# ReLU-squared attention and SwiGLU on one core: the sums of squares of the norm, taken in f32 on ScalarE and VectorE and closed by one matmul

## The chip, the cores and the metric

One core of a Trainium2 chip runs the whole kernel. The metric is the device time of one execution in microseconds, as the median of several runs. Engines are named as the profile names them: PE (TensorE, with PEld for its weight loads), DVE (VectorE), ACT (ScalarE), POOL (GpSimd), SP (SyncE).

## The reference

Eight batches of twelve heads, 448 positions, head size 64. The attention has no softmax: the scores are rectified, squared and divided by the length. Its output, put back into 3584 rows of 768, goes through an RMS norm and a gated feed-forward block without biases (d_ff 1536).

```python
scores = (q @ k.T) / sqrt(64)
attn = maximum(scores, 0) ** 2 / 448
x = (attn @ v) with heads side by side          # 3584 x 768
rms = sqrt(mean(x * x, axis=-1) + 1e-6)
xn = x / rms * rms_g
out = (silu(xn @ w_gate) * (xn @ w_val)) @ w_out
```

All inputs and the output are f32 in memory; the kernel computes its matmuls in bf16 with f32 sums.

## The kernel before, in words

**Layout.** Features lie on partitions: the attention output of a batch is a tile xT of 128 partitions x 6 feature blocks x 448 positions (a block is a pair of heads). The six blocks of a batch come in three **visits** of two blocks each (`visit_aux`): a visit multiplies the rectified and squared scores by V (psAV, L823, 28 matmuls) into a PSUM tile of two banks. One engine then copies that tile, scaled, into xT in bf16 (L850 on DVE or L848 on ACT), and DVE squares the copy in bf16 (L853) into a tile of squares. Within a visit, between the two parts of its V matmuls, four matmuls make scores of the next visit (psR, L737).

**Order.** Nothing in the program waits for "what is ready": a planner in Python (`Planner`) writes one fixed order for each engine. It keeps an estimated time for each engine, gives each task (a copy, a rectification, a square) a cost per engine, and picks the task or matmul that can start first by these estimates. The engines then run their lists in that order, with semaphores where data or a buffer demands it, so a wait that the planner did not count holds everything behind it on that engine. A task's data are given as tokens (`need`), and a PSUM bank counts as free when the task that was given the bank's release ends.

**PE in two halves.** Most matmuls use 64 of the 128 contraction rows, so that two run side by side: half 0 on the lower and half 1 on the upper 64 rows. A segment (`Seg`) is a sum over several slots, half 0 first, then half 1 added to the same PSUM tile; `slot` (L139) issues them, and while half 1 works on one segment half 0 works on the next. The feed-forward blocks (psg, psv), the output projection (psO) and the sums of squares (psSS) of batches 1 to 7 are such segments. Work that is not a segment is put between slots as an insert (`ins`, `do_ins`): the score units psS (L716), one matmul in each half, are.

**PSUM.** Four single banks serve psg, psv, psO and psSS; two double banks (`wide`) serve psS, psR and psAV, so that a score unit needs one of the two to be free. A psS or psR tile is freed by its rectification on ACT (L661) or DVE (L659); a psAV tile was freed by its copy to xT. The squares of the rectified scores (L667) run on DVE, and for batch 1 the planner could also choose POOL.

**Norm.** After the last visit of a batch, `norm_seg` puts a segment of six slots (one per feature block, weights all ones) ahead in PE's stream: 12 matmuls of 64 rows x 448 positions that sum the squares over all features. ACT takes the logarithm and the exponential (L903, L907) for the reciprocal root, DVE makes xn (L922), and the feed-forward block of the batch starts with it. While that goes on, PE works on the output projection (psO) of batches finished earlier. Batch 0 is done in two halves of 224 positions whose sums (L948) are matmuls of their own.

Of the kernel before, what the change touches and what calls it, by code (L numbers as in the profile page):

```python
# [8 lines left out]
FP32 = mybir.dt.float32  # L9
BF16 = mybir.dt.bfloat16  # L10
# [44 lines left out]
class Planner:  # L55
# [6 lines left out]
    def __init__(self, nc, tc, banks, wide, warm):  # L62
        self.nc, self.tc, self.banks, self.wide, self.warm = nc, tc, banks, wide, warm
        self.free = {"act": 1300.0, "dve": 1500.0, "pool": 1300.0, "sp": 1300.0}
        self.tasks, self.seq = [], 0
        self.t = [1100.0, 1100.0]
        self.mode = "row"
        self.ins = [[], []]
        self.aux = None
        self.cur, self.next0, self.q8 = None, [], []  # L70
        self.stream = []
        self.units, self.auxes = [], []
        self.behind = mybir.DependencyInfo(
            mybir.DependencyClass.Sync, mybir.DependencyReason.DATA
        )
# [138 lines left out]

    def half(self, h):
        t = self.t[h]
        if self.ins[h]:
            return t, lambda: self.do_ins(h)
        if self.aux is not None:
            if h == 0 and not self.ins[1]:  # L220
                return max(self.t), self.do_aux
            return None
        if h == 1:
            if not self.q8:
                return None
            seg = self.q8[0]
            if seg.count[1] == 0:
                if seg.fin[0] is None:
                    return None
                return max(t, seg.fin[0]), lambda: self.slot(1, seg)  # L230
            return t, lambda: self.slot(1, seg)
        return self.choose(t)

    def do_ins(self, h):
        self.row()
        w, emit, cb = self.ins[h].pop(0)
        s = self.t[h]
        emit()
        TRACE.append((s, w / 2.4 + 2.5, "pe%d" % h, "score"))
        self.t[h] = s + w / 2.4 + 2.5  # L240
        if cb:
            cb(s + w / 2.4 + self.PSUM)
# [11 lines left out]
    def choose(self, t):  # L254
        self.auxes = [a for a in self.auxes if not a.void()]
        self.warm()
        for a in self.auxes:
            r = a.ready()
            if r is not None and r <= t:
                return t, lambda: self.set_aux(a)  # L260
        s = self.stream_next(t)
        u = None
        if self.units and not any(a.holds() for a in self.auxes):
            u = self.units[0].ready()
        if u is not None and u <= t and (self.units[0].due() or s is None or s[0] > t):
            return t, self.begin_unit
        if s is not None and s[0] <= t:
            return t, lambda: self.slot(0, s[1])
        times = [s[0]] if s is not None else []
        if u is not None:  # L270
            times.append(u)
        for a in self.auxes:
            r = a.ready()
            if r is not None:
                times.append(r)
        if self.warm() and (not times or min(times) > t + 250.0):
            return t, self.filler
        if not times:
            return None
        at = min(times)  # L280
        return at, lambda: self.skip(at)
# [4 lines left out]
    def set_aux(self, a):  # L286
        self.auxes.remove(a)
        self.aux = a

    def begin_unit(self):  # L290
        self.units.pop(0).begin()
# [8 lines left out]
    def run(self):  # L300
        while True:
            p = None
            for h in (0, 1):
                c = self.half(h)
                if c is not None and (p is None or c[0] < p[0]):
                    p = c
            e = self.engine_next()
            if p is None and e is None:
                break
            if e is not None and (p is None or e[3] <= p[0]):  # L310
                self.run_task(*e[1:])
            else:
                p[1]()
        left = (len(self.stream), len(self.q8), len(self.units), len(self.auxes), len(self.tasks))
        assert not any(left) and self.cur is None, left


# [7 lines left out]
def kernel(  # L325
# [11 lines left out]
    nc = tc.nc  # L337
# [38 lines left out]
    def act_cost(n, per=0.8333):  # L376
        return 172.0 + per * n

    def dve_cost(n, per=1.0417):
        return 156.0 + per * n  # L380
# [260 lines left out]
            return None if any(x is None for x in toks) else latest(toks)  # L641

    live = {"r": 0}
    xTs, x2s, rstds, xns, hTs = {}, {}, {}, {}, {}
    subs = [Sub(0, 0, HALF, 0.0), Sub(0, HALF, HALF, 0.0)]
    subs += [Sub(b, 0, S, 0.0 if b < 2 else PACE) for b in range(1, B)]

# [2 lines left out]
    def rectify(sub, ps, bank, w, ready, put):  # L650

        got = {}
        tok = Tok()

        def relu(e):
            r = apool.tile([P, 2, S], BF16, name="r", tag="r")
            got["r"] = r
            if e == "dve":
                nc.vector.tensor_relu(out=r[:, :, :w], in_=ps[:, :, :w])  # L659
            else:  # L660
                nc.scalar.activation(out=r[:, :, :w], in_=ps[:, :, :w], func=ACT.Relu)  # L661
            put(r, tok)

        def square(e):
            r = got["r"]
            eng = nc.vector if e == "dve" else nc.gpsimd
            eng.tensor_tensor(out=r[:, :, :w], in0=r[:, :, :w], in1=r[:, :, :w], op=ALU.mult)  # L667

        a = pl.task(
            PRIO_R, {"act": act_cost(2 * w), "dve": dve_cost(2 * w)}, relu, [Tok(ready)],  # L670
            None, free_bank(bank),
        )
        cost = {"dve": dve_cost(2 * w, 0.52)}
        if sub.b == 1:
            cost["pool"] = 156.0 + 1.75 * 2 * w
        pl.task(PRIO_R, cost, square, [a], tok)

    class Unit:
# [14 lines left out]
        def begin(self):  # L693
            sub, n = self.sub, self.sub.n
            bank = take_wide()
            ps = bank.take("psS")
            live["r"] += 1
            ends = []
            total = 2 * len(self.parts)
            w = n * len(self.parts)  # L700

            def put(r, tok):
                for j, c, o in self.parts:
                    sub.r[j, c] = (r, o, tok)

            def cb(t):
                ends.append(t)
                if len(ends) == total:
                    rectify(sub, ps, bank, w, max(ends), put)

            t = qkT[sub.b]
            for hh in range(2):
                prt = (low, high)[hh]
                for j, c, o in self.parts:
                    def emit(hh=hh, prt=prt, j=j, c=c, o=o):
                        nc.tensor.matmul(  # L716
                            out=ps[:, hh, o : o + n], lhsT=t[prt, j, 0, c * P : (c + 1) * P],
                            rhs=t[prt, j, 1, sub.q0 : sub.q0 + n], start=True, stop=True,
                        )
                    pl.ins[hh].append((n, emit, cb))  # L720

    def rest_ready(sub, k):
        r = [sub.qk(2 * k), sub.qk(2 * k + 1)]
# [39 lines left out]
    def visit_aux(sub, k, then, after):  # L763
# [36 lines left out]
        def run(s):  # L800
# [38 lines left out]
            sub.visited = k + 1  # L839
            if (b, 0) not in xTs:  # L840
                xTs[b, 0] = xpool.tile([P, KT, S], BF16, name="xT", tag="xT")
                x2s[b] = npool.tile([P, KT, S], BF16, name="x2", tag="x2", bufs=2)
            xT, x2 = xTs[b, 0], x2s[b]
            at = (slice(None), slice(ja, jb + 1), slice(q0, q0 + n))

            def copy(e):
                if e == "act":
# [1 line left out]
                else:  # L849
                    nc.vector.tensor_scalar_mul(out=xT[at], in0=ps[:, :, :n], scalar1=inv_attn)  # L850

            def squared(e):
                nc.vector.tensor_tensor(out=x2[at], in0=xT[at], in1=xT[at], op=ALU.mult)  # L853

            c = pl.task(
                1, {"act": act_cost(2 * n), "dve": dve_cost(2 * n)}, copy,
                [Tok(end - w + n / 2.4 + pl.PSUM)], None, free_bank(bank),
            )
            x = pl.task(1, {"dve": dve_cost(2 * n, 0.52)}, squared, [c])
            sub.x2[ja] = sub.x2[jb] = x  # L860
            if k == HP // 2 - 1:
                if b:
                    pl.stream.insert(0, norm_seg(sub))
                if b > 1 and ffn_done[b - 1].t is not None:
                    table["now"] = "norm"
                    pl.task(0, {"act": 1283.0}, lambda e: nc.scalar.preload_act_table_set(NORM_SET) and None, [c])
                finish(sub)
# [12 lines left out]

    table = {"now": "norm"}

    def norm_seg(sub):
        b, n, q0 = sub.b, sub.n, sub.q0
        seg = Seg(
            n, lambda i: (0, ones_bf[:], x2s[b][:, i, q0 : q0 + n]), lambda i: [sub.x2[i]],
            bank={}, name="psSS", done=lambda bk, t: norm_scale(sub, bk, t),
        )
        seg.n, seg.begin = KT, None
        return [seg]  # L890

    def norm_scale(sub, bk, ready):
        b, n, q0 = sub.b, sub.n, sub.q0
# [388 lines left out]
```

## Time and profile before

| what | value |
|---|---|
| median of 7 runs (lowest, highest) | 449.76 us (449.14, 451.13) |
| the profiled execution's own time | 449.15 us |
| its span, first to last instruction | 447.3 us |
| granted PE clock, mean | 0.997 |
| xT copies of 896 elements per partition | 18 on DVE, 3 on ACT |
| squares of xT (L853), 896 elements | 21 on DVE, 620 ns each |
| squares of r (L667) on POOL, batch 1 | 5, 1769 ns each |
| visits of batches 1 to 7 | 21, of which 7 are a batch's last |

The span is cut by the profile into rows: a row gives the start, the duration, the engine, the line, the operation with its tiles, and in brackets how long the engine had been idle and what released it. Rows of matmuls give modelled ends, and they overlap: in a row "x12" the duration covers all twelve. The profiled execution lies 0.61 us below the median of the runs, and 1.85 us of it lie outside the span.

### The profile page before, as it was taken

Reading aid. Unit: us, or ns where it says so; the run is one execution under the profiler, and the core shown is the slowest. Engines: PE = TensorE matmul, PEld = TensorE weight load, DVE = VectorE, ACT = ScalarE, POOL = GpSimd, SP = SyncE. Lnnn points to the kernel's source line nnn. Section 1 sums busy time; section 2 is a strip of 40 time slices with the busy share of each in tenths; the row PEclk is TensorE's granted clock in tenths of the full one; section 3 lists DMA queues with packets and bytes.
Section 4 is the critical chain, followed back from the end, with each engine's and each line's share of the span. In section 5 each row is a group of like instructions: output and inputs, shape, how many; then the busy total and the mean of one; then the engine's idle time right before and its main releaser. Section 6 shows DMA issues by size and latency. Waiting matters only on the chain.

```text
span 447.3 us, 12371 instructions
## 1 busy us (share of the span) xinstructions
PE 439.0 (98%) x5513; PEld 293.2 (66%) x5513; DVE 252.0 (56%) x410; ACT 239.7 (54%) x339; POOL 88.6 (20%) x105
## 2 busy tenths in 40 slices
PE   8999899999999999999999999999999999999996
PEld 6677687765578655765578655765568755666696
DVE  3799776328934666476743766377753676232200
ACT  4787455437843576556634477456634567342222
POOL 8644746430252000620043000100000000000000
PEclk9999999999999999999999999999999999999998
DMA  9999999999999940999039960563003200020023
GB/s 100 186 196 204 202 192 130 178 183 148 146 96 181 152 73 2 96 188 108 1 44 180 190 85 1 71 135 63 1 1 107 72 2 1 1 72 1 2 72 107
DMA packets 134053, 44.45 MB, mean 99 GB/s; under 512 B 105776, under 2 KB 130544, under 8 KB 134000
## 3 DMA queue, kind: packets, MB, share of 16 engines
q0 software_dynamic: 94624, 24.39, 58.3%
q1 hardware_dynamic: 39344, 19.27, 25.2%
q8 instruction: 43, 0.70, 0.7%
q14 instruction: 10, 0.08, 0.1%
q10 hardware_dynamic: 32, 0.01, 0.0%
HBM read 48.76 MB, written 11.01 MB: 134 GB/s over the span
## 4 chain that ended last, share of the span: by engine, by line
PE 93%; DVE 3%; ACT 1%; DMA 1%; issue 1%; POOL 0%; ACTq 0%; POOLq 0%
PE psO L139 25%; PE psv L139 24%; PE psg L139 24%; PE psAV L823 9%; PE psS L716 6%; PE psSS L139 2%; PE psT L582 1%; PE psR L737 1%; DVE xn L922 1%; DMA kb<-in_k_dram 1%; PE psB L1231 1%; DVE r L667 1%; DVE r L659 0%; ACT r L661 0%; ACT qkT L599 0%
## 5 line engine op out<-in xcount | busy, mean ns | idle before, releaser
L139 PE MATMUL psg<-xn,wg_sb 64*128 64x448 bf16 (+1 forms) x1296 | 170.9, 329 | 1.4 <-DVE xn L922 1.2
L139 PE MATMUL psv<-xn,wv_sb 64*128 64x448 bf16 (+1 forms) x1296 | 167.7, 328 | 0.0
L139 PE MATMUL psO<-wo_sb,hT 64*128 64x384 bf16 (+3 forms) x1368 | 141.0, 320 | 0.1
L661 ACT ACTIVATE r<-psS 128x896 bf16<-128x896 f32 x120 | 107.2, 920 | 34.9 <-PE psS L716 31.7
L139 PEld LDWEIGHTS <-hT 64*128 64x128 bf16 x1368 | 101.1, 94 | 23.5 <-issue 2.5
L139 PEld LDWEIGHTS <-wg_sb 64*128 64x128 bf16 x1296 | 86.5, 94 | 44.2 <-issue 6.0
L139 PEld LDWEIGHTS <-wv_sb 64*128 64x128 bf16 x1296 | 85.1, 94 | 39.3 <-issue 2.1
L667 DVE TENSOR_TENSOR r<-r 128x896 bf16<-128x896 bf16 (+1 forms) x166 | 99.7, 620 | 19.0 <-ACT r L661 18.0
L997 DVE TENSOR_TENSOR hT<-sil,psv 128x448 bf16<-128x448 bf16 x96 | 59.5, 619 | 60.0 <-PE psv L139 57.6
L984 ACT ACTIVATE sil<-psg 128x448 bf16<-128x448 f32 x96 | 52.2, 544 | 53.4 <-PE psg L139 53.0
L1075 ACT COPY ost<-psO 128x384 f32<-128x384 f32 (+3 forms) x51 | 24.4, 478 | 61.5 <-PE psO L139 61.5
L716 PE MATMUL psS<-qkT 64*128 64x448 bf16 (+1 forms) x324 | 55.1, 329 | 0.7 <-ACT r L661 0.2
L922 DVE SCALAR_TENSOR_TENSOR xn<-xT,g_sb,rstd 128x448 bf16<-128x448 bf16 (+1 forms) x54 | 32.3, 666 | 29.7 <-ACT rstd L907 29.7
L823 PE MATMUL psAV<-r,vb 64*64 64x448 bf16 (+1 forms) x756 | 43.5, 335 | 0.5 <-issue 0.2
L458 POOL DMA_DIRECT2D vb<-in_v_dram x18 | 13.8, 808 | 137.3 <-PE psO L139 98.7
L488 POOL DMA_DIRECT2D kb<-in_k_dram x42 | 31.8, 813 | 28.1 <-DMA qb<-in_q_dram 20.2
L850 DVE TENSOR_SCALAR xT<-psAV 128x896 bf16<-128x896 f32 (+1 forms) x21 | 21.5, 1025 | 27.2 <-PE psAV L823 27.2
L661 ACT ACTIVATE r<-psR 128x896 bf16<-128x896 f32 (+1 forms) x22 | 19.1, 867 | 30.7 <-PE psR L737 30.6
L659 DVE TENSOR_SCALAR r<-psS 128x896 bf16<-128x896 f32 x24 | 26.0, 1087 | 15.1 <-PE psS L716 15.1
L823 PEld LDWEIGHTS <-vb 64*64 64x64 bf16 x756 | 18.5, 105 | 20.9 <-issue 8.4
L716 PEld LDWEIGHTS <-qkT 64*128 64x128 bf16 x324 | 20.5, 94 | 12.8 <-issue 1.9
L853 DVE TENSOR_TENSOR x<-xT 128x896 bf16<-128x896 bf16 (+1 forms) x27 | 15.4, 569 | 7.4 <-ACT xT L848 7.4
(40 smaller groups left out, 177.3 us busy)
## 6 DMA issues: line engine op xcount, KB each, us to landing
vb<-in_v_dram POOLq DMA_DIRECT2D x14, 384.0 KB, 7.7
kb<-in_k_dram POOLq DMA_DIRECT2D x45, 96.0 KB, 10.8
qb<-in_q_dram POOLq DMA_DIRECT2D x6, 672.0 KB, 17.3
out_dram<-ost SPq DMA_DIRECT2D x7, 336.0 KB, 3.5
wo_sb<-in_moe_w_out_dram POOLq DMA_DIRECT2D x2, 1152.0 KB, 21.2
out_dram<-ost SPq DMA_DIRECT2D x8, 288.0 KB, 4.3
out_dram<-ost SPq DMA_DIRECT2D x8, 240.0 KB, 4.2
wg_sb<-in_moe_w_gate_dram POOLq DMA_DIRECT2D x4, 384.0 KB, 12.5
```

The source lines that it names most:

```text
L139: mm = self.nc.tensor.matmul(out=seg.bank["tile"][:, off : off + seg.w], lhsT=lhsT[prt], rhs=rhs[prt], start=(seg.first and h == 0 and i = ...
L488: lambda o=o, i=i: nc.gpsimd.dma_start(out=o, in_=i),
L659: nc.vector.tensor_relu(out=r[:, :, :w], in_=ps[:, :, :w])
L661: nc.scalar.activation(out=r[:, :, :w], in_=ps[:, :, :w], func=ACT.Relu)
L667: eng.tensor_tensor(out=r[:, :, :w], in0=r[:, :, :w], in1=r[:, :, :w], op=ALU.mult)
L716: nc.tensor.matmul(out=ps[:, hh, o : o + n], lhsT=t[prt, j, 0, c * P : (c + 1) * P], rhs=t[prt, j, 1, sub.q0 : sub.q0 + n], start=True, st ...
L823: mm = nc.tensor.matmul(out=ps[hh * D : (hh + 1) * D, jj, :n], lhsT=vt[prt, 2 * (ja + jj) + hh, u * D : (u + 1) * D], rhs=r[prt, hh, o : o ...
L850: nc.vector.tensor_scalar_mul(out=xT[at], in0=ps[:, :, :n], scalar1=inv_attn)
L922: nc.vector.scalar_tensor_tensor(out=xn[:, kt, q0 : q0 + n], in0=xTs[b, 0][:, kt, q0 : q0 + n], scalar=g_sb[:, kt : kt + 1], in1=rstd[:, q ...
L984: nc.scalar.activation(out=s[:, :m], in_=ps[:, :m], func=ACT.Silu)
L997: nc.vector.tensor_tensor(out=h[:, fbs[0] : fbs[-1] + 1, o : o + n], in0=s[:, :m].rearrange("p (f s) -> p f s", s=n), in1=ps[:, :m].rearra ...
L1075: nc.scalar.copy(out=ost[:, c0 : c0 + w], in_=ps[:, :w])
```

## The change

The bf16 squares on DVE and the six-slot segment go away for batches 1 to 7. In their place ACT squares the psAV tile itself, straight from PSUM, in f32 (`x2f`, two tiles in turn); DVE adds the blocks up in f32 (`acc`), and the last add writes bf16 (`ssum`). So a batch has three Square instructions and five adds of 448 elements. The sum over partitions is one matmul in each half, put between slots as an insert by a new list of the planner (`sneaks`), half 1 at a time set by when half 0 is expected to be done. A psAV tile now has two readers, copy and Square, and its bank counts as free when both tasks have ended. The squares of r for batch 1 lose POOL as a choice. Batch 0 stays as it was.

```diff
-        if sub.b == 1:
-            cost["pool"] = 156.0 + 1.75 * 2 * w
...
-            c = pl.task(
-                1, {"act": act_cost(2 * n), "dve": dve_cost(2 * n)}, copy,
-                [Tok(end - w + n / 2.4 + pl.PSUM)], None, free_bank(bank),
-            )
-            x = pl.task(1, {"dve": dve_cost(2 * n, 0.52)}, squared, [c])
-            sub.x2[ja] = sub.x2[jb] = x
+            told = Tok(end - w + n / 2.4 + pl.PSUM)
+            left = [1 if b == 0 else 2]
+
+            def over(t):
+                left[0] -= 1
+                if not left[0]:
+                    bank.free = t + 60.0
...
+            c = pl.task(1, {"act": act_cost(2 * n), "dve": dve_cost(2 * n)}, copy, [told], None, over)
...
+                def squared(e):
+                    got["x2"] = npool.tile([P, 2, S], FP32, name="x2f", tag="x2f", bufs=2)
+                    nc.scalar.activation(
+                        out=got["x2"][:], in_=ps[:, :, :n], func=ACT.Square, scale=inv_attn
+                    )
+
+                x = pl.task(1, {"act": act_cost(2 * n)}, squared, [told], None, over)
+                for i in range(2):
+                    if ja + i == 0:
+                        continue
+
+                    def summed(e, i=i):
+                        first = got["x2"][:, 0, :] if ja + i == 1 else accs[b][:]
+                        to = x2s[b] if ja + i == HP - 1 else accs[b]
+                        nc.vector.tensor_tensor(out=to[:], in0=first, in1=got["x2"][:, i, :], op=ALU.add)
+
+                    sub.sum = pl.task(1, {"dve": dve_cost(n)}, summed, [x] + ([sub.sum] if ja + i > 1 else []))
             if k == HP // 2 - 1:
                 if b:
-                    pl.stream.insert(0, norm_seg(sub))
+                    pl.sneaks.append(norm_sum(sub))
...
+    def norm_sum(sub):
+        b, n, got = sub.b, sub.n, {}
+
+        def ready():
+            r, f = latest([sub.sum]), bank_ready()
+            return None if r is None or f is None else max(r, f)
+
+        def half(h):
+            prt = (low, high)[h]
+            if h:
+                pl.wait_for(got["mm"])
+            got["mm"] = nc.tensor.matmul(
+                out=got["tile"][:, :n], lhsT=ones_bf[prt], rhs=x2s[b][prt], start=h == 0, stop=h == 1,
+            ).ins
...
+                pl.ins[1].append((n, lambda: half(1), lambda t: norm_scale(sub, got, t), t - pl.PSUM + pl.HAND))
+
+            pl.ins[0].append((n, lambda: half(0), first, 0.0))
```

Every choice of the planner after the first such visit is made anew, so the lists of PE, ACT and DVE differ in many places; the numbers of matmuls, rectifications, table loads and transfers stay the same but for the parts named.

More of the change, by code (lines that the diff above doesn't have):

```diff
@@ L71, in __init__ @@
         self.stream = []
-        self.units, self.auxes = [], []
+        self.units, self.auxes, self.sneaks = [], [], []
         self.behind = mybir.DependencyInfo(
@@ L216, in half @@
         t = self.t[h]
-        if self.ins[h]:
-            return t, lambda: self.do_ins(h)
+        if self.ins[h] and (self.ins[h][0][3] <= t or self.aux is not None):
+            return max(t, self.ins[h][0][3]), lambda: self.do_ins(h)
         if self.aux is not None:
@@ L224, in half @@
             if not self.q8:
-                return None
+                return (self.ins[1][0][3], lambda: self.do_ins(1)) if self.ins[1] else None
             seg = self.q8[0]
@@ L235, in do_ins @@
         self.row()
-        w, emit, cb = self.ins[h].pop(0)
-        s = self.t[h]
+        w, emit, cb, at = self.ins[h].pop(0)
+        s = max(self.t[h], at)
         emit()
@@ L260, in choose @@
                 return t, lambda: self.set_aux(a)
+        for a in self.sneaks:
+            r = a.ready()
+            if r is not None and r <= t:
+                return t, lambda: self.sneak(a)
         s = self.stream_next(t)
@@ L271, in choose @@
             times.append(u)
-        for a in self.auxes:
+        for a in self.auxes + self.sneaks:
             r = a.ready()
@@ L288, in set_aux, with sneak @@
         self.aux = a
+    def sneak(self, a):
+        self.sneaks.remove(a)
+        a.run()
     def begin_unit(self):
@@ L313, in run @@
                 p[1]()
-        left = (len(self.stream), len(self.q8), len(self.units), len(self.auxes), len(self.tasks))
+        left = (len(self.sneaks), len(self.stream), len(self.q8), len(self.units), len(self.auxes), len(self.tasks))
         assert not any(left) and self.cur is None, left
@@ L643 @@
     live = {"r": 0}
-    xTs, x2s, rstds, xns, hTs = {}, {}, {}, {}, {}
+    xTs, x2s, accs, rstds, xns, hTs = {}, {}, {}, {}, {}, {}
     subs = [Sub(0, 0, HALF, 0.0), Sub(0, HALF, HALF, 0.0)]
@@ L719, in emit @@
                         )
-                    pl.ins[hh].append((n, emit, cb))
+                    pl.ins[hh].append((n, emit, cb, 0.0))
     def rest_ready(sub, k):
@@ L841, in run @@
                 xTs[b, 0] = xpool.tile([P, KT, S], BF16, name="xT", tag="xT")
-                x2s[b] = npool.tile([P, KT, S], BF16, name="x2", tag="x2", bufs=2)
-            xT, x2 = xTs[b, 0], x2s[b]
-            at = (slice(None), slice(ja, jb + 1), slice(q0, q0 + n))
+                if b == 0:
+                    x2s[b] = npool.tile([P, KT, S], BF16, name="x2", tag="x2")
+                else:
+                    accs[b] = npool.tile([P, S], FP32, name="acc", tag="acc")
+                    x2s[b] = npool.tile([P, S], BF16, name="ssum", tag="ssum", bufs=2)
+            xT = xTs[b, 0]
+            at = (slice(None), slice(ja, jb + 1), slice(q0, q0 + n))
+            told = Tok(end - w + n / 2.4 + pl.PSUM)
[4 more added lines that the diff above has]
+                    bank.free = t + 60.0
             def copy(e):
@@ L850, in copy, with squared @@
                     nc.vector.tensor_scalar_mul(out=xT[at], in0=ps[:, :, :n], scalar1=inv_attn)
-            def squared(e):
-                nc.vector.tensor_tensor(out=x2[at], in0=xT[at], in1=xT[at], op=ALU.mult)
-            c = pl.task(
-                1, {"act": act_cost(2 * n), "dve": dve_cost(2 * n)}, copy,
-                [Tok(end - w + n / 2.4 + pl.PSUM)], None, free_bank(bank),
-            )
-            x = pl.task(1, {"dve": dve_cost(2 * n, 0.52)}, squared, [c])
-            sub.x2[ja] = sub.x2[jb] = x
+            c = pl.task(1, {"act": act_cost(2 * n), "dve": dve_cost(2 * n)}, copy, [told], None, over)
+            if b == 0:
+                def squared(e):
+                    nc.vector.tensor_tensor(out=x2s[b][at], in0=xT[at], in1=xT[at], op=ALU.mult)
+                x = pl.task(1, {"dve": dve_cost(2 * n, 0.52)}, squared, [c])
+                sub.x2[ja] = sub.x2[jb] = x
+            else:
+                got = {}
+                def squared(e):
+                    got["x2"] = npool.tile([P, 2, S], FP32, name="x2f", tag="x2f", bufs=2)
[11 more added lines that the diff above has]
+                    sub.sum = pl.task(1, {"dve": dve_cost(n)}, summed, [x] + ([sub.sum] if ja + i > 1 else []))
             if k == HP // 2 - 1:
                 if b:
-                    pl.stream.insert(0, norm_seg(sub))
+                    pl.sneaks.append(norm_sum(sub))
                 if b > 1 and ffn_done[b - 1].t is not None:
@@ L881, with run, first @@
     table = {"now": "norm"}
[L883 to L890, printed above, removed]
+    def norm_sum(sub):
[10 more added lines that the diff above has]
+            ).ins
+        def run():
+            got["bank"] = take_bank()
+            got["tile"] = got["bank"].take("psSS")
+            def first(t):
+                pl.ins[1].append((n, lambda: half(1), lambda t: norm_scale(sub, got, t), t - pl.PSUM + pl.HAND))
+            pl.ins[0].append((n, lambda: half(0), first, 0.0))
+        return Aux("sums", "row", ready, run)
     def norm_scale(sub, bk, ready):
```

## The prediction

> **What bounds the kernel now.** I read the page's totals and its chain first: if one engine carries the chain, only that engine's instructions and its waits count.
>
> ```profile
> span 447.3 us, 12371 instructions
> PE 439.0 (98%) x5513; PEld 293.2 (66%) x5513; DVE 252.0 (56%) x410; ACT 239.7 (54%) x339; POOL 88.6 (20%) x105
> ...
> PE 93%; DVE 3%; ACT 1%; DMA 1%; issue 1%; POOL 0%; ACTq 0%; POOLq 0%
> ```
>
> PE carries 93% of the chain; DVE and ACT are half idle. Then PE's waits: what is left for other engines to spoil or to give back.
>
> ```profile
> PE psB L1231 <- DVE busy_bf L389: 1.2, 1, 1.2
> PE psg L139 <- DVE xn L922: 1.2, 2, 0.6
> PE psT L582 <- DMA kb<-in_k_dram: 0.9, 1, 0.9
> PE psS L716 <- ACT r L661: 0.2, 1, 0.2
> ```
>
> PE waits some 4 us in all, and never for a square or a sum. So DVE time taken away gains nothing, PE slots taken away gain in full, and each new wait on PE costs in full, because PE's order is fixed. Now the rows of what is exchanged (x count, then busy us and mean ns):
>
> ```profile
> L850 DVE TENSOR_SCALAR xT<-psAV 128x896 bf16<-128x896 f32 x18 | 19.7, 1092 | 25.2 <-PE psAV L823 25.2
> L139 PE MATMUL psSS<-x,ones_bf 64*128 64x448 bf16 x84 | 18.1, 349 | 0.0
> L853 DVE TENSOR_TENSOR x<-xT 128x896 bf16<-128x896 bf16 x21 | 13.0, 620 | 6.0 <-ACT xT L848 6.0
> L848 ACT ACTIVATE xT<-psAV 128x896 bf16<-128x896 f32 x3 | 2.8, 917 | 8.2 <-PE psAV L823 8.2
> ```
>
> **What it gains.** The 349 ns are the length of one matmul; the pace is read from the timeline of a norm: psSS of one half start at 183.40, 183.59, 183.78, so a slot is 0.19 us, and the other half works beside it on psO. A norm takes six slots of each half and will take one: 5 x 0.189 = 0.95 us, in seven norms **-6.6 us**.
>
> **What it costs: visits in the middle of a batch.** This is the timeline after a visit that is not the last of its batch:
>
> ```profile
> 165.84 0.92 ACT L661 ACTIVATE r<-psR 128x896 bf16<-128x896 f32 x1 [1.10 <-PE psR L737]
> 166.38 0.74 PE L139 MATMUL psv<-xn,wv_sb 64*128 64x448 bf16 x6
> 166.50 1.09 DVE L850 TENSOR_SCALAR xT<-psAV 128x896 bf16<-128x896 f32 x1 [2.06 <-PE psAV L823]
> 166.96 0.35 PE L716 MATMUL psS<-qkT 64*128 64x448 bf16 x2
> 167.72 0.35 PE L716 MATMUL psS<-qkT 64*128 64x448 bf16 x2
> ```
>
> The first psS takes the bank of psR, the second the bank of psAV. The copy of psAV ends at 167.59, and the second psS starts at 167.72: nothing to spare. In the change psAV has two readers. The code gives copy and Square the same token, as if they ran side by side; in the instruction lists of the changed program the Square on ACT waits for DVE's semaphore at the count that the copy gives, in all 18 visits whose copy is on DVE. So it runs behind the copy, and the second psS waits for the Square.
>
> The trace has one reader for each psAV tile, so no row shows two engines reading one bank together. The Trainium skill's PSUM page (PSUM — Partial Sum Buffer, "PSUM bank collisions raise a hardware error") speaks against the plan: two engines may not touch one bank in the same partitions at once, reads against reads included. By that rule the two run in turn, as the lists have it and the sum here does; without it they would overlap, which is the third case below.
>
> The price: the Square is ACT's pass over 896 elements of PSUM, for which the xT row on ACT has 917 ns (f32 output costs nothing there: ost copies of 384 f32 take 480 ns, sil of 448 bf16 544). A hand-over between engines shows as 0.03 us (xT on ACT ends at 77.95, its square on DVE starts at 77.98); I take 0.05. The second psS can start 1.09 + 0.05 + 0.92 + 0.05 = 2.11 us after the copy's start, and stood at 1.22: **0.89 us** of PE. The lists after have the same 6 + 2 + 6 slots between psAV and that psS in ten visits, and 12 + 2 + 12 half-width ones in batch 1's second (psS 1.23 us behind the copy). Two others (batches 4 and 6, first visits) have 28 slots, 2.6 us, in between, and batch 1's first copies on ACT: no wait. 11 x 0.89 = **+9.8 us**. Ends: 0.03 per hand-over gives 0.85 and 9.4; 0.15 at each, what a restart of PE and its weight load (94 ns in their row) might add, gives 1.09 and 12.0. Nothing hides it: PE is in order, and ACT sits idle 0.8 us in front of the Square.
>
> **Visits at the end of a batch.** There the sum is the wait. The change puts half 0 of psSS after 36 psO (24 before) in batches 2, 3 and 5.
>
> ```profile
> 181.28 2.35 PE L139 MATMUL psO<-wo_sb,hT 64*128 64x384 bf16 x24
> 181.39 1.09 DVE L850 TENSOR_SCALAR xT<-psAV 128x896 bf16<-128x896 f32 x1 [1.06 <-PE psAV L823]
> 183.40 0.35 PE L139 MATMUL psSS<-x,ones_bf 64*128 64x448 bf16 x1
> 184.45 1.06 PE L139 MATMUL psO<-wo_sb,hT 64*128 64x384 bf16 x10
> ```
>
> psO goes at (1.06 - 0.32)/9 = 0.082 us, so twelve more put half 0 at 2.01 + 0.98 = 2.99 us after the copy's start. The data: copy 1.09, Square 0.92, two f32 adds, four hand-overs and a weight load of 0.09. An add of 448 f32 in SBUF is no row; with 2 bytes at twice the pace 448 elements of a square take 386 ns, xn with its f32 operand 680; I take 619 (hT, 448 elements with one f32 operand), the nearest. That makes 3.54: **0.55 us** each, 1.7 in three (nothing with adds of 386 and hand-overs of 0.03; 1.1 each with 680 and 0.15). In batches 4 and 6 half 0 stays where it was, 2.98 behind the copy, and an ost copy of 256 (0.42) stands between the two adds: 3.75, so 0.77 each, 1.5 in two (0.2 and 1.2 by the same ends). In batches 1 and 7 copy and Square are both on ACT, planned one behind the other, and half 0 has 37 and 44 psO ahead: nothing. Together **+3.2 us** (0.4 to 5.7). Half 1 follows six or seven psO later, 0.5 us, against 0.19 of half 0's stream and its hand-over: no wait counted.
>
> **What costs nothing.** ACT's 21 Squares (19.3 us) and DVE's balance (35 adds less 21 squares, 8.7 us) lie beside PE. Here too the skill has a rule against the change (ScalarE: Activation LUTs, "Rules for kernel authors"): simple multiplications belong on VectorE; the rows agree, 620 against 917 ns, but neither engine sets the end, so by it the sum would move only if ACT became late elsewhere. Queued behind the waiting Square on ACT are rectifications and sil; sil frees psg's bank, of which there are four, each filled in 12 slots x 0.0945 = 1.13 us a half. ACT is late by 0.9 + 0.9 us and PE by 0.9, so 0.9 us of lag remain against about 2.3 until the bank is wanted: covered; uncovered, up to 0.4 us in ten visits, 4 us. Batch 1's five squares go from POOL (1769 ns each) to DVE, 3.1 us, in 50 to 77 us of the span, where DVE is busy 19.0 of 27.0: covered, else up to 3.1. POOL then issues its kb and qb loads without the 10.5 us that it waited for r; no PE wait there is for a load, so no gain. Table loads stay 18, and what follows the norm is ready relative to half 0 as before.
>
> **Sum**, against the profiled execution's own 449.15: - 6.6 + 9.8 + 3.2 = **455.6**. That execution lies 0.61 below the median of the runs, so as a median **456.2 us**, 1.4% slower.
>
> **Rivals.**
> 1. *Stalls with knock-on* (0.12): ACT's lateness reaches psg or psv banks, or a third psS behind its rectification; the ceilings above (12.0, 5.7 and up to 4) reach 465; a third of the way there is 459. For it: r<-psR, Square and two rectifications are now one row of work on ACT. Against: PE, late itself, gives ACT time.
> 2. *Part of the stalls is taken back* (0.12): a stall on PE lets DVE and ACT finish other things that PE would have met. With half of the 13.0 us gone: 449.7. Against: PE had next to no waits to give back.
> 3. *The Square runs beside the copy* (0.08), the other side: it decides if the Square's start lies before the copy's end. Then the second psS finds its bank at 1.09 + 0.1, as before, half 0's data at 2.5 of 2.99, no stall is left, and the 6.6 us stay: 443.2. The lists speak against it.
>
> That the change does not do what it says is not likely: the lists have 14 psSS matmuls in place of 84, and 21 Squares.
>
> **Numbers.** The forecast holds 0.68 (453 to 459). The range 451 to 461 takes in the ends of the stalls (-6.6 + 9.4 + 0.4 gives 453.0 as median, -6.6 + 12.0 + 5.7 gives 460.9) and the nearer parts of rivals 1 and 2; outside are rival 3 and the far ends, some 0.17. A measurement tells about 0.2% from no change. Slower by more: the forecast, rival 1 and half of rival 2, 0.87. Within 0.2%: 0.03. Faster: rival 3 and what more than half of the stalls taken back would give, 0.10.
>
> **What will show it.** A wait of PE's psS for ACT's Square, eleven times about 0.9 us, and of psSS (or its weight load) for DVE's last add, five times 0.5 to 0.8; ACT idle in front of each Square until the copy on DVE ends; psSS down to 14 matmuls; PE's busy time down by about 6 us while the span grows. Squares that start with the copy, or eleven waits well under 0.5 us, would prove me wrong; so would long waits of psg for sil.

## The result, and the profile after

The changed kernel takes **453.0 us** (median of 12 runs, 452.41 to 453.33) beside 450.4 us of the kernel before in the same session: ratio **1.0061, 95% interval 1.0048 to 1.0075**. So it is slower, as forecast, and the time lies in the range; but it lost 2.6 us where 6.4 were forecast. The profiled execution took 452.78 us, at a granted clock of 1.0.

Totals and chain of the page after:

```profile
span 451.0 us, 12262 instructions
PE 435.0 (96%) x5443; PEld 305.3 (68%) x5443; DVE 262.8 (58%) x434; ACT 255.7 (57%) x355; POOL 79.9 (18%) x100
...
PE 86%; DVE 5%; ACT 4%; POOL 1%; DMA 1%; issue 1%; ACTq 0%; POOLq 0%
```

PE has 70 matmuls fewer and is busy 4 us less, and still the span is longer: PE's share of the chain fell from 93% to 86%, and DVE and ACT took it. PE's waits say where (waiting line, what it waited for; us in total, times, longest):

```profile
PE psS L722 <- ACT x2f L881: 7.8, 11, 0.7
...
PE psSS L930 <- DVE ssum L893: 1.1, 5, 0.3
```

Eleven waits for the Square and five for the last add: the forecast counts, to the number. And the timeline of one visit, batch 2's first:

```profile
109.34 1.09 DVE L867 TENSOR_SCALAR xT<-psAV 128x896 bf16<-128x896 f32 x1 [1.65 <-PE psAV L829]
...
109.81 0.35 PE L722 MATMUL psS<-qkT 64*128 64x448 bf16 x2
...
110.47 0.92 ACT L881 ACTIVATE x2f<-psAV 128x896 f32<-128x896 f32 x1 [0.87 <-DVE xT L867]
...
111.44 0.37 PE L722 MATMUL psS<-qkT 64*128 64x448 bf16 x2 [0.71 <-ACT x2f L881]
```

The copy ends at 110.43, the Square starts at 110.47 after ACT has stood idle 0.87 us, and the second psS starts 2.10 us behind the copy's start (2.11 forecast). So the forecast stalls are all there. What made up for part of them shows when both traces are laid side by side by the first psAV of each visit. At the last visit of batch 0 the changed kernel lies 0.18 us behind; at the first visit of batch 1 it lies 2.99 us *ahead* (51.90 us into the span against 54.89); from there to the end it loses 6.64 us, against 6.4 forecast. So nearly the whole miss is one step of 3.2 us between 38 and 55 us, before any of the new Squares. (The two profiled executions lie 3.6 us apart, not 2.6: the one of the kernel before, 449.15 us, is 1.3 us under its median. Experiment 2 says where that comes from.) The table of windows shows that stretch (43 to 51 us; its length; busy us and instructions of PE, PEld, DVE, ACT, POOL; then the granted clock, the DMA share and GB/s), the kernel before first:

```profile
43.00:51.00 8.00, 6.41 (x87) 4.50 (x82) 8.00 (x12) 5.37 (x9) 6.58 (x7) 1.00 1.42 198
```

and the changed one:

```profile
43.00:51.00 8.00, 7.94 (x146) 7.06 (x144) 8.00 (x16) 6.23 (x10) 1.62 (x3) 1.00 1.42 197
```

In the kernel before, PE is busy 6.4 of 8.0 us with 87 matmuls; in the changed one 7.9 with 146. DVE is full in both, but gets 12 instructions done in one and 16 in the other; POOL is what differs. The timeline of before there:

```profile
44.54 1.07 DVE L659 TENSOR_SCALAR r<-psS 128x896 bf16<-128x896 f32 x1
44.71 1.67 POOL L667 TENSOR_TENSOR r<-r 128x896 bf16<-128x896 bf16 x1 [0.74 <-DVE r L659]
45.54 1.09 DVE L922 SCALAR_TENSOR_TENSOR xn<-xT,g_sb,rstd 128x224 bf16<-128x224 bf16 x1
46.35 1.82 POOL L667 TENSOR_TENSOR r<-r 128x896 bf16<-128x896 bf16 x1
46.55 1.86 DVE L922 SCALAR_TENSOR_TENSOR xn<-xT,g_sb,rstd 128x224 bf16<-128x224 bf16 x1
...
48.47 0.27 PE L139 MATMUL psg<-xn,wg_sb 64*128 64x224 bf16 x2 [0.55 <-DVE xn L922]
```

An xn piece of 224 elements takes 0.44 us elsewhere (439 is the shortest of the six in this stretch, 442 their median). Here one that starts during a POOL square takes 1.09 us and the next 1.86; each ends some 0.25 us after the POOL square does (46.63 after 46.38, 48.41 after 48.17). The rectification at 44.54, which reads one operand and that from PSUM, keeps its 1.07 us beside the same POOL square. Two more DVE operations start beside a POOL square and read both inputs from SBUF, squares of r that take 0.61 us elsewhere: at 42.34 us one takes 1.28, at 62.61 one 1.21, and both end 0.48 us after the POOL square. A product that reads one input from PSUM (hT, at 41.81) keeps its 0.61. PE then waits for xn.

### The profile page after: what moved, and what is told of

Same layout as the page of the kernel before. It is cut to its first block, busy times and chain, and to the rows that moved or that the text cites. A ratio compares the mean times of both kernels' runs of the same rounds, so it can differ in the third digit from the quotient of the medians.

```text
span 451.0 us, 12262 instructions
## 1 busy us (share of the span) xinstructions
PE 435.0 (96%) x5443; PEld 305.3 (68%) x5443; DVE 262.8 (58%) x434; ACT 255.7 (57%) x355; POOL 79.9 (18%) x100
## 4 chain that ended last, share of the span: by engine, by line
PE 86%; DVE 5%; ACT 4%; POOL 1%; DMA 1%; issue 1%; ACTq 0%; POOLq 0%
PE psv L139 23%; PE psg L139 23%; PE psO L139 22%; PE psAV L829 9%; PE psS L722 6%; DVE xT L867 4%; ACT x2f L881 3%; DMA kb<-in_k_dram 1%; PE psT L590 1%; PE psR L743 1%; DVE ssum L893 1%; PE psSS L930 1%; POOL kb L466 1%; PE psB L1284 1%; POOL qb L454 0%
## 5 line engine op out<-in xcount | busy, mean ns | idle before, releaser
L139 PE MATMUL psg<-xn,wg_sb 64*128 64x448 bf16 (+1 forms) x1296 | 173.9, 329 | 0.1
L139 PE MATMUL psv<-xn,wv_sb 64*128 64x448 bf16 (+1 forms) x1296 | 172.4, 328 | 0.0
L139 PE MATMUL psO<-wo_sb,hT 64*128 64x384 bf16 (+3 forms) x1368 | 136.1, 320 | 0.1
L139 PEld LDWEIGHTS <-wg_sb 64*128 64x128 bf16 x1296 | 93.6, 94 | 35.8 <-issue 3.5
L139 PEld LDWEIGHTS <-hT 64*128 64x128 bf16 x1368 | 103.7, 94 | 17.9 <-issue 2.5
L139 PEld LDWEIGHTS <-wv_sb 64*128 64x128 bf16 x1296 | 92.2, 94 | 34.2 <-issue 2.5
L1128 ACT COPY ost<-psO 128x384 f32<-128x384 f32 (+3 forms) x45 | 21.5, 477 | 45.7 <-PE psO L139 45.3
L975 DVE SCALAR_TENSOR_TENSOR xn<-xT,g_sb,rstd 128x448 bf16<-128x448 bf16 (+1 forms) x54 | 30.3, 628 | 8.1 <-ACT rstd L960 7.8
L881 ACT ACTIVATE x2f<-psAV 128x896 f32<-128x896 f32 x21 | 19.2, 917 | 15.7 <-DVE xT L867 15.7
```

Of the source, the lines that this page charges most:

```text
L139: mm = self.nc.tensor.matmul(out=seg.bank["tile"][:, off : off + seg.w], lhsT=lhsT[prt], rhs=rhs[prt], start=(seg.first and h == 0 and i = ...
L881: nc.scalar.activation(out=got["x2"][:], in_=ps[:, :, :n], func=ACT.Square, scale=inv_attn)
L975: nc.vector.scalar_tensor_tensor(out=xn[:, kt, q0 : q0 + n], in0=xTs[b, 0][:, kt, q0 : q0 + n], scalar=g_sb[:, kt : kt + 1], in1=rstd[:, q ...
```

## The experiments

The theory after the result: POOL's squares of r hold up DVE's xn, so taking them off POOL gains some 3 to 4 us, which the forecast priced at nothing; the rest of the sum holds. The rival: POOL has no part in it, and the stalls cost less than their length, because PE's lateness is made up for elsewhere. A second question: is the stall the price of two readers of psAV, or of a plan that was not told of it? Each ratio is to the kernel before on the same chip; each time is a median.

**1. The kernel before, POOL not a choice.** This one part of the change alone:

```diff
-        if sub.b == 1:
-            cost["pool"] = 156.0 + 1.75 * 2 * w
```

> The kernel before with one edit: POOL is no longer a choice for batch 1's squares. Theory (POOL's squares hold up DVE's two-operand work beside them): the six xn of batch 0's second half, 4.4 us of DVE between 45.5 and 50.4 before, take some 2.3, PE's waits for xn go, and the first visit of batch 1 comes 3.2 us earlier, as in the changed kernel: 447.2 us against 450.4, ratio 0.993. Rival (the changed kernel gained those 3.2 us by its new order from batch 1 on, not by POOL): this edit alone gives 450.4, ratio 1.000.

Measured: **446.33 us** (446.01 to 446.52), 4.05 below the 450.38 beside it, ratio 0.9915 (0.990 to 0.993). PE no longer waits for xn, and the six pieces are all short (row of xn from 41 to 51 us: shortest, median, longest ns):

```profile
L920 DVE SCALAR_TENSOR_TENSOR xn<-xT,g_sb,rstd x6: 446/451/451, 44.7 to 47.0; 128x224 bf16<-128x224 bf16 x6
```

The gain is real, and its own.

**2. The changed kernel with POOL as a choice again.** The same two lines put back.

> The changed kernel with POOL given back as a choice for batch 1's squares. Theory: the 3.2 us come back, 456.2 us, ratio 1.013, which is the sum of the prediction without any gain from POOL; xn of batch 0's second half take 0.6 to 0.9 us again. Rival (order, not POOL): 453, ratio 1.006.

Measured: **456.25 us** (455.46 to 457.79), ratio 1.014 (1.0119 to 1.0161). This is the change without the POOL edit, and it comes out at the 456.2 of the forecast. The longest xn piece is 1862 ns again; PE's waits for the Square are 7.8 us in eleven, as in the changed kernel. The rival falls: without the POOL edit the stalls cost what was forecast.

These medians hold one thing more, the clock. In the profiled execution of this run (457.10 us) the granted clock falls to one half for 3.4 us, right behind the stretch in which PE was short of xn (columns as above):

```profile
47.00:50.60 3.60, 2.16 (x23) 1.19 (x23) 3.60 (x8) 2.01 (x4) 2.45 (x4) 1.00 1.47 196
50.60:54.00 3.40, 3.40 (x37) 3.25 (x36) 1.03 (x2) 0.79 (x2) 2.11 (x4) 0.50 1.34 204
```

PE starts 37 matmuls there; in the profile of the kernel before (449.15 us) it starts 69 in the same window, at a clock of 1.00. Such a dip lowers the mean clock of an execution by 0.004. Of the 35 executions of the kernel before that were timed beside these experiments, 17 have a mean clock of 0.993 to 0.996 and take 450.1 to 451.1 us; the other 18 have 0.997 or more and a median of 449.3. Of the 60 executions of versions without squares on POOL, two have a mean under 0.997. So about 1.2 us of the 4.05 of experiment 1 go with the clock. At an equal clock POOL's squares cost 2.7 to 2.9 us: 449.3 less 446.33, and in the two traces, where batch 1's first visit comes at 54.89 and 52.22 us and the spans are 447.3 and 444.6. That the dip follows from PE's shortage is likely by these counts, but no run sets the one without the other.

**3. The kernel before, the five squares moved to DVE in an unchanged plan.** Experiment 1 also made the planner's later choices anew. Here the order of everything else stays:

```diff
-            eng = nc.vector if e == "dve" else nc.gpsimd
+            eng = nc.vector
```

> The kernel before, with its plan untouched: every instruction stands where it stood, but the five squares of r that POOL ran are issued on DVE, although the planner still counts them as POOL's. Theory (a POOL square holds up the DVE operations that read two tiles in SBUF until it ends): the xn pieces of 224 all take about 0.44 us, none 1.86, PE's waits for xn in the stretch 43 to 51 us shrink, and the time falls by 2 to 3.5 us, to about 447 to 448.5 (the DVE list gets five squares of about 1.2 us or less that it was not planned for, so not the whole 4.05 us of the first experiment). Rival (the first experiment gained by the new order of its instructions, not by POOL's absence): the xn pieces stay slow or the five unplanned squares on DVE cost as much as they save, 450 to 452.

Measured: **447.68 us** (447.38 to 448.15), ratio 0.9947 (0.9931 to 0.9962). The xn pieces take 443 to 447 ns. DVE was given five squares that nobody had planned, and the time still fell by 2.6 us (from 450.3): it is POOL's activity beside DVE, not the new order, that costs (at the clock of this run, 0.998 or more, the gain is 1.6 us, 449.3 less 447.68). The other 1.35 us of experiment 1 come with the new order. POOL's queue, which here has no squares to hold up its loads, is not what gains: PE waits once for a load in either trace, at the start (0.88 us at 6.71 before, 1.21 us at 6.79 here).

**4. The changed kernel, Square planned behind the copy.** One token: the planner is told that the Square needs the copy `c`, not just the psAV tile.

```diff
-                x = pl.task(1, {"act": act_cost(2 * n)}, squared, [told], None, over)
+                x = pl.task(1, {"act": act_cost(2 * n)}, squared, [c], None, over)
```

> The changed kernel with one token changed: the planner is told that the Square needs the copy. Square and copy run in turn as before, but PE's order is written for it. Theory (the planner's order, not the turn itself, costs): PE's waits for the Square (7.8 us in 11 places) and for the last add (4.1 us) go to under 1 us in all, and the time falls by 8 to 13 us to 440 to 445, ratio 0.977 to 0.988. Rival (the psAV bank held 0.9 us longer is itself the price, since a score unit needs one of two banks): the waits move elsewhere and the time stays at 450 to 453, ratio 1.000 to 1.006.

Measured: **442.83 us** (442.32 to 443.09), ratio 0.9836 (0.982 to 0.9851). The Square still runs behind the copy, on the same tile with the same 917 ns, but no wait of PE for it is left:

```profile
PE psB L1284 <- DVE busy_bf L397: 1.2, 1, 1.2
PE psT L590 <- DMA kb<-in_k_dram: 0.7, 1, 0.7
PE psS L722 <- ACT r L669: 0.2, 1, 0.2
```

So the stall is the price of an estimate that had the two readers side by side. When the planner knows, it puts other slots ahead of that psS.

**5. The same, Square of xT instead of psAV**, so that the PSUM tile has one reader again and its bank comes free with the copy.

```diff
-            left = [1 if b == 0 else 2]
+            left = [1]
...
-                        out=got["x2"][:], in_=ps[:, :, :n], func=ACT.Square, scale=inv_attn
+                        out=got["x2"][:], in_=xT[at], func=ACT.Square
...
-                x = pl.task(1, {"act": act_cost(2 * n)}, squared, [told], None, over)
+                x = pl.task(1, {"act": act_cost(2 * n)}, squared, [c])
```

> The changed kernel, but the Square on ACT reads the bf16 copy xT in SBUF, not psAV; it needs the copy in the plan too, and the bank is free when the copy ends, as in the kernel before. Theory: no PE wait for a Square is left, and the full 6.6 us of the sums and 3.2 us of POOL are kept: 440 to 442 us, ratio 0.978 to 0.981. If the held bank is a price of its own, this one is clearly faster than the one with the token alone; if only the plan was, the two are within 1 us. Rival (the extra 19 us on ACT cost time by themselves): 446 or more.

Measured: **442.81 us** (442.49 to 444.33), ratio 0.9844 (0.9824 to 0.9864). The same as 4, and a little above what was expected: a bank held 0.92 us longer costs nothing when it is planned.

**Where 3 us went.** Experiment 1 less the forecast's 6.6 us of slots is 439.7; 4 and 5 stand 3.1 above it. In their traces one half of PE stands idle 0.98 us once in each of the stretches after batch 3's and batch 5's last visit. The next five runs ask why. Theory: the chain from the last visit's copy through square, sums and exponentials to xn has grown, and there it sets the pace.

**6. The squares back on DVE in bf16**, with the f32 sums and the single matmul kept.

```diff
...
-                    got["x2"] = npool.tile([P, 2, S], FP32, name="x2f", tag="x2f", bufs=2)
-                    nc.scalar.activation(
-                        out=got["x2"][:], in_=ps[:, :, :n], func=ACT.Square, scale=inv_attn
-                    )
+                    got["x2"] = npool.tile([P, 2, S], BF16, name="x2f", tag="x2f", bufs=2)
+                    nc.vector.tensor_tensor(out=got["x2"][:], in0=xT[at], in1=xT[at], op=ALU.mult)
...
-                x = pl.task(1, {"act": act_cost(2 * n)}, squared, [told], None, over)
+                x = pl.task(1, {"dve": dve_cost(2 * n, 0.52)}, squared, [c])
```

> The changed kernel, but DVE squares the copied xT in bf16 (planned behind the copy) as the kernel before did, and the f32 sums and the one matmul stay. The chain to the norm is some 0.3 us shorter than with ACT's Square of 917 ns (620 for 917). Theory (in the stages behind the last visits of batches 1, 3, 5, 7 the end of that chain sets the time): 441.5 to 442.5, a little under the 442.8 of the two planned forms of ACT's Square. Rival (what is missing from the 6.6 us has another cause): 442.8 or, since DVE has 21 x 0.62 us more to do, up to 444.

Measured: **440.06 us** (440.01 to 440.14), ratio **0.9776 (0.976 to 0.9793)**: better than expected, and the best version of all, faster than both kernels. Against experiment 1 it gains 6.27 us, nearly the 6.6 that the slots alone are worth. The two timelines behind batch 3's last visit show why more than 0.3 us was at stake. With ACT's Square (experiment 5; first psAV of the visit at 175.70):

```profile
179.12 0.95 ACT L881 ACTIVATE x2f<-xT 128x896 f32<-128x896 bf16 x1
179.99 0.56 DVE L1130 COPY ost<-psO 128x384 f32<-128x384 f32 x1 [0.81 <-PE psO L139]
180.47 0.61 DVE L893 TENSOR_TENSOR acc<-acc,x2f 128x448 f32<-128x448 f32 x1
...
183.27 0.63 ACT L956 ACTIVATE rstd<-psSS,eps_col 128x448 f32<-128x448 f32 x1 [0.85 <-PE psSS L930]
```

With DVE's squares (experiment 6; first psAV at 175.41):

```profile
178.81 0.62 DVE L881 TENSOR_TENSOR x2f<-xT 128x896 bf16<-128x896 bf16 x1
179.46 0.62 DVE L891 TENSOR_TENSOR acc<-acc,x2f 128x448 f32<-128x448 f32 x1
...
182.03 0.64 ACT L954 ACTIVATE rstd<-psSS,eps_col 128x448 f32<-128x448 f32 x1
```

The Square takes 0.95 us instead of 0.62, and the order puts an output copy on DVE ahead of the adds, so that the first add starts 0.40 us behind the Square's end instead of 0.03. The logarithm starts 7.57 us behind the first psAV instead of 6.62: 0.95 us late, nearly as long as the idle half. What the idle half waits for at its end is, by the rows, not xn: the order puts a third psS ahead of psg, and this psS starts at 187.62 us, 0.05 behind a rectification on ACT (186.65, 0.92 us), while the first piece of xn was done at 185.24. In 6 psg follows two psS at 186.35. So the late norm acts at least in part through the order that the planner wrote for it; no run holds that order fixed.

**7 and 8. Only one visit's squares moved.** To part the chain from ACT's load: first the last visit of each batch on DVE and the others on ACT, then the complement. The edit puts 6's branch or 5's behind a condition on the visit; this is 7's, and 8 has `k < HP // 2 - 1` in its place:

```diff
...
+                    if k == HP // 2 - 1:
+                        got["x2"] = npool.tile([P, 2, S], BF16, name="x2b", tag="x2b", bufs=2)
+                        nc.vector.tensor_tensor(out=got["x2"][:], in0=xT[at], in1=xT[at], op=ALU.mult)
+                    else:
+                        got["x2"] = npool.tile([P, 2, S], FP32, name="x2f", tag="x2f", bufs=2)
+                        nc.scalar.activation(out=got["x2"][:], in_=xT[at], func=ACT.Square)
...
```

> From the version whose Square reads xT: the first two visits of a batch are squared by ACT as there, the last visit's two blocks by DVE in bf16. Measured so far: all squares on ACT 442.8, all on DVE 440.06, although the shorter chain alone was expected to leave 441.5 to 442.5. In the trace with ACT's Square a PE half stands idle 0.98 us some 12 us after the first psAV of batches 4 and 6, in the one with DVE's squares it does not. Theory (the chain from the last visit's copy to xn is the whole difference): 440.0 to 440.7. Rival (ACT's 21 Squares press on the other work of ACT and DVE, whichever visit they belong to): two thirds of the difference stay, 441.5 to 442.3.

> The complement: the first two visits are squared by DVE in bf16, the last visit's two blocks by ACT from xT in f32. Theory (the chain behind the last visit): 442.3 to 443.0, as with all squares on ACT. Rival (the load of ACT): only a third of the difference, 440.7 to 441.2.

Measured: last visit on DVE **440.41 us** (440.26 to 440.6), ratio 0.9793 (0.9774 to 0.9812); last visit on ACT **442.27 us** (442.15 to 442.62), ratio 0.9834 (0.9815 to 0.9854), 0.03 under the theory's bounds and well outside the rival's. Seven of the 21 Squares make most of the difference; the other fourteen make 0.35 us (7 against 6). From batch 3's last visit to batch 5's, the first psAVs lie 100.76 us apart in 7 and in 6, but 101.76 in 8 and in 5; and the logarithm behind batch 3's starts 6.62 us after the first psAV in 7, 7.57 in 8.

**9. Three slots instead of one.** From 5: four blocks summed as there, the last visit's two squared on DVE and sent to PE as they are, so that no add stands in the chain and the sum is three matmuls in each half.

```diff
...
-                out=got["tile"][:, :n], lhsT=ones_bf[prt], rhs=x2s[b][prt], start=h == 0, stop=h == 1,
+                out=got["tile"][:, :n], lhsT=ones_bf[prt], rhs=x2s[b][prt, i, :],
+                start=h == 0 and i == 0, stop=h == 1 and i == 2,
...
```

> From the version whose Square reads xT: the first four blocks are squared on ACT and summed on DVE as there, but the last visit's two blocks are squared in bf16 on DVE and go to TensorE as they are, so the sum over partitions is three matmuls in each half instead of one. The chain behind the last copy is then 0.62 us of squares instead of 0.92 of Square and 1.25 of two adds, less some 0.4 us for two more slots: about 1.1 us shorter for 7 x 0.38 = 2.6 us more of TensorE. Theory (the norm's chain sets the time behind the last visits of batches 1, 3, 5, 7): the four odd batches give back 0.7 us each or so and the three even ones cost 0.38, in sum 440 to 442. Rival (the chain does not set the time): 442.8 + 2.6 = 445.4.

Measured: **445.29 us** (445.02 to 445.48), ratio 0.9892 (0.9875 to 0.9909): a miss for the theory's number and a hit for the rival's. The chain did get shorter (logarithm at 5.83 us behind batch 3's first psAV), but below the 6.6 of experiment 7 nothing more is to be had, while every added slot is paid: from batch 3 to batch 5 it takes 101.67 us, 7's 100.76 plus two norms of 0.38 plus 0.15. So a longer chain to the norm costs that one microsecond, and a shorter one gives nothing. The run lies 4.9 us above 7; the slots make 2.7 of these, the rest is not settled.

**10. The last visit's blocks left out of the sum.** From 5: the norm is summed from four blocks of six, so that it need not wait for the last visit.

```diff
...
-                x = pl.task(1, {"act": act_cost(2 * n)}, squared, [c])
+                if k < HP // 2 - 1:
+                    x = pl.task(1, {"act": act_cost(2 * n)}, squared, [c])
...
```

> From the version whose Square reads xT: the last visit's two blocks are left out of the sum of squares, so the norm is computed from four blocks of six and the output is not the reference's; the slot, the exponentials and xn stay. The norm's chain then no longer waits for the last visit. Theory (that chain eats some 3 of the 6.6 us): 439.0 to 440.5, near the 446.33 - 6.6 = 439.7 that the removed slots alone would give. Rival (the 3 us go elsewhere, to the planner's order or to other waits): 442 to 443.

Measured: **449.81 us** (449.54 to 451.09), ratio 0.9997 (0.9985 to 1.0009). Neither expectation: the run says nothing on the chain, because the planner, free to do the norm early, put its logarithm and exponential among the silus, and ACT changes its table back and forth. Of the groups of ACT, L957, L961 and L1038 (logarithm, exponential, silu) have five table loads each, the last of them:

```profile
L1038 ACT ACT_TABLE_LOAD x5 | 6.4, 1283 | 0.1
```

These are 15 loads more than in any other run here, 19.2 us of ACT, and PE waits 4.9 us for silus. Inconclusive, and a warning on leaving work out where a scheduler decides.

## Why the prediction was wrong in size, point by point

- *Visits in the middle of a batch, 11 x 0.89 = 9.8:* right. Eleven psS start late, 0.875 us each by the trace, 9.6. That the Square runs behind the copy was read in the lists, and all 18 Squares whose copy is on DVE wait for it (15.7 us of idle ACT). So the two readers go in turn, as the lists had it; that is the order which the rule cited in the prediction (the Trainium skill, PSUM — Partial Sum Buffer, "PSUM bank collisions raise a hardware error") asks for, but no run here shows what two readers at once would do.
- *Last visits, 3.2:* right in place, too large. Half 0 of psSS is 0.44 us late in batches 2, 3 and 5 and 0.48 in 4 and 6, 2.3 in all. The adds were priced right (619 forecast, 615 to 626 measured); the hand-overs were not, as half 0 starts 3.43 us behind the copy's start in batch 2, where the sum gave 3.54.
- *Slots, -6.6:* right. The clean pair, experiments 1 and 6, gives -6.27 with the adds on DVE included.
- *"POOL then issues its kb and qb loads ...; no PE wait there is for a load, so no gain", and the squares' move "covered, else up to 3.1":* **this step failed**. It asked where the squares go, in 50 to 77 us, and whether DVE has room; not what POOL's squares do to DVE while they run, from 41.5 to 67.0 us (three of the five before 50). In this trace they hold up, until they end, all four DVE operations with both inputs in SBUF that start more than 0.1 us before that end. As medians that is worth 4.05 us in the kernel before (experiment 1), 2.6 without any replanning (3), and 3.3 between the changed kernel and the one with POOL (456.25 - 453.0, experiment 2); at an equal clock 2.7 to 2.9, 1.6 and 2.6 (455.6, the median of the three executions at 0.997 or more, less 453.0). The rest goes with the clock, for which the prediction had no term. That 453.0 lies in the range at all is luck: the range was made for the ends of the stalls and the nearer parts of rivals 1 and 2, not for this gain. It could be read before the change: the only PE wait for xn, "1.2, 2, 0.6", is in the very lines that the prediction quotes, and the xn group's pieces of 224 range from 439 to 1865 ns. The 1.2 us were the small part; the larger is one half of PE working alone, which the waits don't list, as the other half keeps PE busy (87 matmuls against 146 from 43 to 51 us).
- *Sum:* 450.4 - 4.05 (POOL, experiment 1) - 6.3 (slots, 6 against 1) + 9.6 + 2.3 makes 452.0 (450.4 - 4.05 is experiment 1's own time, so its share of the clock cancels); 453.0 was measured. The last 1.0 us I place only by the trace: single halves of PE idle 0.2 to 0.5 us at a time behind the last visits of batches 3, 4 and 5. No run tests it.
- *Rivals:* the sum of 3 (443.2) was reached (442.83), but by another way than it had: the Square never ran beside the copy, and POOL's gain is in it. It was enough to tell the planner (experiment 4). Knock-on (1) and stalls taken back (2) did not show: from batch 1's first visit on the loss was 6.64.
- *"Simple multiplications belong on VectorE", "by it the sum would move only if ACT became late elsewhere":* the Trainium skill's rule (ScalarE: Activation LUTs, "Rules for kernel authors") did bear on the time once the stalls were gone. Seven Squares of 0.95 us on ACT in place of 0.62 on DVE cost 1.9 us where they stand in the chain to the norm (8 against 7); the fourteen others, which load ACT twice as much, cost 0.35 (7 against 6).

## What to carry to other kernels

Price each edit by what the removed work did to its neighbours, too: take the stretch in which it ran and look for operations of one shape with two durations. Half of a busy engine can be idle without a wait in the list, so compare instructions done in equal windows as well. When a buffer gets a second reader, tell the scheduler the order in which the readers will really run: one token was worth 10.2 us here (453.0 to 442.83), more than the whole change.

## What the runs showed of the hardware

- A POOL product of 896 bf16 elements (1.67 to 1.99 us) holds a DVE operation with two inputs in SBUF until it ends: xn of 224 elements took 1.09 and 1.86 us instead of 0.44, a square of 896 took 1.28 and 1.21 instead of 0.61. A DVE rectification from PSUM beside it kept its 1.07 us. The Trainium skill (SBUF — State Buffer, "Who interferes with whom") says that a DVE instruction with two SBUF inputs contends with a GpSimd instruction that reads SBUF, and that one with at most one such input, outside the modes in which DVE uses two ports, does not; these rows agree with both.
- In experiment 2 the granted clock stood at 0.50 for 3.4 us behind 3.6 us in which PE had started 23 matmuls, where the changed kernel started 74; in the kernel before, with 24 matmuls there, the profiled execution kept 1.00. So such a stretch can be followed by a dip but need not be.
- ACT's Square of 896 elements costs 917 ns from PSUM and 948 from SBUF in bf16, so reading SBUF is not the faster way there; and it needed no table load of its own (18 loads before and after).
